# Retention and two FFN layers on one core: early steps in another order on GpSimd, ScalarE and VectorE

## The chip, the cores and the metric

The kernel runs on one core of one Trainium2 chip. The metric is the device time of one execution in microseconds; the median of three timed runs is used. A profile of one further execution gives the trace.

## The reference

The inputs q, k and v have 4 batches, 8 heads, 768 positions and 64 columns per head, in float32. A retention layer comes first, then two feed-forward layers without biases.

```
gamma = 1 - 2 ** (-5 - arange(H));  scale = 1 / sqrt(D)
for t in range(S):
    state = gamma * state + outer(k[t], v[t])
    y[t] = scale * q[t] @ state
x = y as (3072, 512)
h = x @ w_in;   x = max(0.01 * h, h) @ w_out           # 512 -> 2048 -> 512
h = x @ w2_in;  x = h * sigmoid(1.702 * h) @ w2_out
```

The weights arrive as 64-bit values and are turned into float32 on the chip.

## The kernel before

**Retention in chunks.** The positions are cut into chunks of 128. A step `s` is one chunk of one batch; there are 24, six to a batch (`c` is the chunk within its batch). `a_load(s)` fetches four rows of 256 KB: q transposed, k transposed, k by rows and v. `a_scale(s)` multiplies q by its decay on GpSimd (L298; on VectorE for step 0, L296). `a_scores(s)` makes the score matmuls (L278) and the mask product on VectorE (L281). For the steps below `TURNED` the rows of k are not loaded: TensorE transposes k (L286) and VectorE multiplies by the key decay (L289). For the other steps GpSimd does that product on the loaded rows (L300). The last chunk of a batch needs no rows of k. `a_out(s)` makes the state matmuls (L312), the values matmuls (L318), the matmuls with the carried state (L324) and the product that carries the state on (L327, VectorE, from PSUM). `a_store(s)` copies the output from PSUM (L340, ScalarE); for the first four steps, which are the first block of tokens of the FFN, it casts it (L343) and subtracts on GpSimd (L151), because the FFN works with a high and a low part of each float32.

**First FFN beside it.** From step `FIRST` = 6 on, three or four pieces of the first block's FFN run in every step (`ffn_pieces`, L229; three matmuls a contraction piece, four pieces for one of 16 column groups `m`). The weights of column group `m` pass through these instructions: the load of the raw words (`load_raw`, L161 and L163, sync queue), two on ScalarE (`words_scalar`, L173 and L174), four on VectorE (`words_vector`, L177, L179, L181, L183), a rounding addition on GpSimd (`round_up`, L192), the cast to the high part on ScalarE (L154) and the low part by subtraction on VectorE (L151), the last two in `finish`. `starts[m]` is the step whose pieces first use `m` (6, 7, 8, 9, 10, 11, 13, ...); the words are made two steps ahead of it and `finish` comes one step ahead. The raw words have a ring of three places, the made words a ring of two, the step inputs a ring of four.

**Order.** Every engine and every DMA queue runs its instructions in the order in which the program lists them. The order of the steps' parts is written out by hand in the loop at the end of `retention`. Everything after retention (the other blocks of the first FFN, its output layer and the second FFN) does not change.

**Start.** `qdec`, the decay of q, is made from two short rows (`qrows`) with one product on TensorE (L380) and copied by ScalarE (L381). `keep_warm` issues matmuls on zeros (L376), whose result nobody uses.

Of the kernel before, what the change touches and what calls it, by code (L numbers as in the profile page):

```python
# [11 lines left out]
F32 = mybir.dt.float32  # L12
BF16 = mybir.dt.bfloat16
F32R = mybir.dt.float32r
U32 = mybir.dt.uint32
# [6 lines left out]
P = 128  # L22
# [65 lines left out]
def retention_two_ffn(ctx: ExitStack, tc: tile.TileContext, qkv, consts, small, w1i, w1o, w2i, w2o, scratch, out):  # L88
    nc = tc.nc
# [21 lines left out]
    def ring(places, *dims):  # L111
        while True:
            for area, at in places:
                yield area.view(at, *dims)

    def run_of(area, n, step, at=0):
        return [(area, at + step * k) for k in range(n)]
# [22 lines left out]
    x0 = xs_a[0].view(0, NP, 2, TB)  # L140
# [6 lines left out]
    a_ring = ring(run_of(early, 2, 2), 512)  # L147
    raw, conv, wt = {}, {}, {}

    def subtract(o, x, y, e=nc.vector):  # L150
        e.tensor_tensor(out=o, in0=x, in1=y, op=ALU.subtract)  # L151

    def split(hi, lo, src, eng=nc.vector):
        nc.scalar.copy(out=hi, in_=src)  # L154
        subtract(lo, src, hi.bitcast(F32), eng)
# [3 lines left out]
    def exchanged(d, s):  # L159

        nc.sync.dma_start(out=d[:, :2], in_=s[:, :2])  # L161
        for r, t in halves:
            nc.sync.dma_start(out=d[r, 2:], in_=s[t, 2:])  # L163

    def load_raw(m):
        raw[m] = t = next(raw_ring).bitcast(U32)
        exchanged(t.rearrange("p (k f) two -> p k f two", k=NP),
                  w1i[m].bitcast(U32).rearrange("p (k f two) -> p k f two", k=NP, two=2))

    def words_scalar(f, low, high):  # L170


        nc.scalar.activation(out=f.bitcast(F32), in_=high.bitcast(F32), func=AF.Abs)  # L173
        nc.scalar.activation(out=low.bitcast(I32), in_=low, func=AF.Copy, scale=2.0**-29)  # L174
# [11 lines left out]
    def words(f, low, high):  # L186
        words_scalar(f, low, high)
        for step in words_vector:
            step(f, high)

    def round_up(f, low, e=nc.vector):
        e.tensor_tensor(out=f.bitcast(I32), in0=f.bitcast(I32), in1=low.bitcast(I32), op=ALU.add)  # L192

    def convert(m):
        t = raw.pop(m)
        a = next(a_ring).bitcast(U32)
        words(a, t[:, :, 0], t[:, :, 1])
        conv[m] = a, t[:, :, 0]

    def finish(m):  # L200
        a = conv.pop(m)[0].bitcast(F32)
        wt[m] = t = home["h1"].view(4 * m, 2, 512)
        split(t[:, 0], t[:, 1], a)
# [8 lines left out]
            x_load(q + 1)  # L212

    PIECES = NP * KF
    FIRST, TURNED = 6, 6
    upto = [PIECES * max(s - FIRST + 1, 0) // (N_STEPS - FIRST) for s in range(N_STEPS)]
    starts = [next(s for s in range(N_STEPS) if upto[s] > NP * m) for m in range(KF)]

# [24 lines left out]
    def retention():  # L243
# [5 lines left out]
        smalls = few.view(3, NC * H + NC * NP)  # L249
# [6 lines left out]
        gdec = smalls[:, NC * H :].rearrange("p (c n) -> p c n", c=NC)  # L256
        mask = mask_t.rearrange("p (n e) i -> p e n i", e=2)
        steps = [(b, c) for b in range(B) for c in range(NC)]
        ins, sc_t = {}, {}
        kv = banks[:, 2, : NP * D].rearrange("p (n d) -> p n d", n=NP)  # L260
        turned = banks[:, 7]
        o = banks[:, 3:5]
# [1 line left out]
        def a_load(s):  # L264
            ins[s] = next(in_ring)
            parts = ((0, 2), (3, 4)) if s < TURNED or steps[s][1] == NC - 1 else ((0, 4),)
            for a, b in parts:
                nc.sync.dma_start(out=ins[s][:, a:b], in_=qkv[s, :, a:b])
# [23 lines left out]
        def a_scale(s):  # L292
            b, c = steps[s]
            q, k = ins[s][:, 0], ins[s][:, 2].rearrange("p (h d) -> p h d", h=H)
            if s == 0:
                nc.vector.tensor_tensor(out=q, in0=q, in1=banks[:, 3], op=ALU.mult)  # L296
            else:
                nc.gpsimd.tensor_tensor(out=q, in0=q, in1=qdec, op=ALU.mult)  # L298
            if s >= TURNED and c < NC - 1:
                nc.gpsimd.tensor_tensor(out=k, in0=k, in1=kdec[:, c].unsqueeze(2).to_broadcast([P, H, D]), op=ALU.mult)  # L300

        def a_out(s):
            b, c = steps[s]
            t = ins.pop(s)
            sm, ks = sc_t.pop(s), t[:, 2].rearrange("p (h d) -> p h d", h=H)
            q = t[:, 0].rearrange("p (n i) -> p n i", n=NP)
            v = t[:, 3].rearrange("p (n f) -> p n f", n=NP)
            if c < NC - 1:
                for n in range(NP):
                    for e in range(2):  # L310
                        r = slice(D * e, D * e + D)
                        nc.tensor.matmul(out=kv[r, n], lhsT=ks[:, 2 * n + e], rhs=v[:, n, r],  # L312
                                         start=(c == 0 and n == 0), stop=True, skip_group_check=True)
            out = lambda n, e: o[D * (e ^ (n >> 1)) : D * (e ^ (n >> 1)) + D, n // 2, n % 2 * P : n % 2 * P + P]
            for n in (0, 2, 1, 3):
                for e in range(2):
                    r = slice(D * e, D * e + D)
                    nc.tensor.matmul(out=out(n, e), lhsT=v[:, n, r], rhs=sm[:, e, n], start=(n % 2 == 0),  # L318
                                     stop=(c == 0), skip_group_check=True)
            if c > 0:  # L320
                for n in (0, 2, 1, 3):
                    for e in range(2):
                        r = slice(D * e, D * e + D)
                        nc.tensor.matmul(out=out(n, e), lhsT=st[c % 2][r, n], rhs=q[r, n], start=False, stop=True,  # L324
                                         skip_group_check=True)
            if c < NC - 1:
                nc.vector.tensor_tensor(out=st[(c + 1) % 2], in0=kv, op=ALU.mult,  # L327
                                        in1=gdec[:, c + 1, :].unsqueeze(2).to_broadcast([P, NP, D]))

        def a_store(s):  # L330
            blk, cc = divmod(s, CPB)
            cols = slice(cc * P, cc * P + P)
            if blk == 1:
                x = x_raw[:, cc // 2, :, cc % 2 * P : cc % 2 * P + P]
            else:
                if cc % 2 == 0:
                    a_store.x = next(x_ring)
                x = a_store.x[:, :, cc % 2 * P : cc % 2 * P + P]

            nc.scalar.copy(out=x.rearrange("p (u m) i -> p u m i", u=2),  # L340
                           in_=o[:, :, : 2 * P].rearrange("p u (m i) -> p u m i", i=P))
            if blk == 0:
                nc.scalar.copy(out=x0[:, :, 0, cols], in_=x)  # L343
                subtract(x0[:, :, 1, cols], x, x0[:, :, 0, cols].bitcast(F32), nc.gpsimd)
            elif blk > 1 and cc % 2:
                nc.sync.dma_start(out=xd0[blk][:, cc // 2], in_=a_store.x)

        ins[0] = next(in_ring)
        nc.scalar.dma_start(out=qrows, in_=consts[0:P:D, H:].rearrange("p n i -> p (n i)"))
        nc.scalar.dma_start(out=smalls, in_=small)  # L350
        nc.sync.dma_start(out=ins[0][:, :2], in_=qkv[0, :, :2])
        nc.sync.dma_start(out=ins[0][:, 3:], in_=qkv[0, :, 3:])
        for n in (1, 2, 3):
# [19 lines left out]
        def keep_warm(n):  # L373

            for _ in range(n):
                nc.tensor.matmul(out=warm, lhsT=idle[:, :P], rhs=idle, start=True, stop=True, skip_group_check=True)  # L376

        pieces = itertools.chain.from_iterable(ffn_pieces(0, m) for m in range(KF))
        keep_warm(4)
        nc.tensor.matmul(out=banks[:, 3], lhsT=half, rhs=qrows, start=True, stop=True, skip_group_check=True)  # L380
        nc.scalar.copy(out=qdec, in_=banks[:, 3])  # L381
        keep_warm(4)
        a_scale(0)
        a_scores(0)
        a_scale(1)
        for s in range(len(steps)):
            if s == 0:
                keep_warm(4)
            if s < FIRST - 1:
                a_scores(s + 1)  # L390
            elif s >= FIRST:
                a_scores(s)
            for m in range(KF):
                if starts[m] == s + 1:
                    finish(m)
            fresh = [m for m in range(KF) if starts[m] == s + 2]
            for m in fresh:
                if m + 2 < KF:
                    load_raw(m + 2)
                convert(m)  # L400
            for _ in range(upto[s] - (upto[s - 1] if s else 0)):
                next(pieces)
            a_out(s)
            for m in fresh:
                round_up(*conv[m], nc.gpsimd)
            if s + 2 < len(steps):
                a_scale(s + 2)
            a_store(s)
            if s + 4 < len(steps):
                a_load(s + 4)  # L410
            if s == 1:
                load_raw(1)
            if s >= len(steps) - 4:
                x_split(1, s - len(steps) + 4)

# [712 lines left out]
```

## Time and profile before

| | |
|---|---|
| timed runs, median (lowest to highest) | 1053.87 us (1053.57 to 1054.02) |
| the profiled execution's own time | 1054.79 us |
| its span | 1053.0 us |
| TensorE busy | 1043.2 us, 99% |
| VectorE busy | 815.4 us, 77% |
| ScalarE busy | 552.7 us, 52% |
| GpSimd busy | 141.4 us, 13% |

The span is the time from the first to the last recorded instruction; the execution's own time has a little around it. Busy times are sums of the records of an engine. Matmuls are pipelined and their ends are modelled, so a busy TensorE is not TensorE at its peak. GpSimd works in the first 126 us, in retention, and again roughly between 580 and 790 us.

### The profile page before, as it was taken

The page shows a single profiled execution, that of the slowest core. Times are in us where ns is not written, and L with a number is a line of the kernel's source. Part 1 is how long each engine was busy: PE and PEld are TensorE (multiplying, and loading weights), DVE is VectorE, ACT ScalarE, POOL GpSimd, SP SyncE. Part 2 cuts the span into 40 slices and gives each one's busy share as a digit, 9 for nine tenths or more (in the row PEclk, how much of TensorE's full clock was granted, in tenths as well). Part 3 has the DMA queues.
Part 4 walks back from the last instruction along what each step waited for, and adds up shares of the span by engine and source line. Part 5 has one row for each costly group of instructions (what it writes and reads, how often), then busy time and mean ns, then how long its engine had stood idle before and what let it go on. Part 6 is the DMA issues. An engine that isn't in the chain of part 4 may idle for free.

```text
span 1053.0 us, 16918 instructions
## 1 busy us (share of the span) xinstructions
PE 1043.2 (99%) x5969; PEld 895.2 (85%) x5969; DVE 815.4 (77%) x1377; ACT 552.7 (52%) x976; POOL 141.4 (13%) x132
## 2 busy tenths in 40 slices
PE   9899999999999999999999999999999999999998
PEld 6677788888788888888888999999999888888886
DVE  4888739877796698788789667676777998887886
ACT  2444436554554554554555666565556564545443
POOL 4666500000000000000000203443510000000000
PEclk9999999999999999999999999999999999999999
DMA  7899667898896523623528855657578735726624
GB/s 256 281 342 363 242 202 236 285 340 304 301 344 237 186 63 108 229 80 130 191 71 310 288 194 184 237 194 257 181 249 269 262 101 128 193 86 150 165 81 80
DMA packets 168185, 221.11 MB, mean 210 GB/s; under 512 B 57634, under 2 KB 109090, under 8 KB 165668
## 3 DMA queue, kind: packets, MB, share of 16 engines
q1 hardware_dynamic: 133232, 173.05, 51.1%
q10 hardware_dynamic: 34868, 46.98, 12.2%
q8 instruction: 47, 0.77, 0.3%
q14 instruction: 38, 0.31, 0.1%
HBM read 135.05 MB, written 84.93 MB: 209 GB/s over the span
## 4 chain that ended last, share of the span: by engine, by line
PE 90%; DMA 4%; DVE 3%; ACT 1%; issue 1%; POOL 1%; ACTq 0%; SPq 0%; DVEq 0%; POOLq 0%
PE psum L786 41%; PE psum L593 22%; PE psum L229 21%; PE psum L278 2%; PE psum L318 2%; DMA wds<-b 2%; DMA h<-qkv 1%; PE psum L324 1%; PE psum L312 1%; DMA wds<-c 1%; PE psum L376 0%; DMA y<-c 0%; DVE b L151 0%; DVE c L1002 0%; DVE c L794 0%
## 5 line engine op out<-in xcount | busy, mean ns | idle before, releaser
L786 PE MATMUL psum<-c,h 128*128 128x512 f32 x1008 | 228.8, 389 | 0.0
L786 PEld LDWEIGHTS psum<-c,h 128*128 128x128 f32 x1008 | 189.3, 188 | 39.2
L786 PE MATMUL psum<-e,h 128*128 128x512 f32 x768 | 179.3, 389 | 0.0
L786 PEld LDWEIGHTS psum<-e,h 128*128 128x128 f32 x768 | 144.1, 188 | 29.9
L229 PE MATMUL psum<-d,h 128*128 128x512 f32 x576 | 136.8, 394 | 0.8 <-ACT e L234 0.8
L229 PE MATMUL psum<-a,h 128*128 128x512 f32 x576 | 131.2, 389 | 0.0
L229 PEld LDWEIGHTS psum<-d,h 128*128 128x128 f32 x576 | 106.7, 188 | 25.1 <-ACT e L234 1.2
L229 PEld LDWEIGHTS psum<-a,h 128*128 128x128 f32 x576 | 108.0, 188 | 22.6 <-issue 0.2
L593 PE MATMUL psum<-c,h 128*128 128x384 f32 x576 | 110.1, 334 | 0.3 <-DVE d L630 0.3
L593 PE MATMUL psum<-b,h 128*128 128x384 f32 x576 | 110.0, 334 | 0.0
L593 PEld LDWEIGHTS psum<-c,h 128*128 128x128 f32 x576 | 100.7, 188 | 0.6 <-DVE d L630 0.6
L593 PEld LDWEIGHTS psum<-b,h 128*128 128x128 f32 x576 | 100.8, 188 | 0.0
L739 ACT CAST c<-b 128x512 fp32r<-128x512 f32 x96 | 59.2, 622 | 57.1 <-DVE c L151 35.6
L613 ACT ACTIVATE d<-psum 128x384 f32<-128x384 f32 x96 | 47.1, 491 | 65.4 <-PE psum L593 57.7
L151 POOL TENSOR_TENSOR a<-a 128x768 f32<-128x768 f32 x7 | 13.2, 1893 | 498.5 <-DMA h<-wds 451.9
L151 DVE TENSOR_TENSOR c<-b,c 128x512 fp32r<-128x512 f32 x96 | 65.4, 689 | 18.8 <-ACT c L739 16.6
L739 ACT CAST e<-a 128x512 fp32r<-128x512 f32 x77 | 47.7, 622 | 43.8 <-PE psum L786 23.0
L234 ACT ACTIVATE e<-psum 128x512 f32<-128x512 f32 x80 | 47.5, 593 | 41.2 <-PE psum L229 38.4
L151 DVE TENSOR_TENSOR h<-h 128x384 fp32r<-128x384 f32 (+3 forms) x88 | 44.0, 535 | 27.7 <-ACT h L154 19.5
L151 DVE TENSOR_TENSOR e<-a,e 128x512 fp32r<-128x512 f32 x77 | 52.2, 684 | 8.3 <-ACT e L739 7.7
L617 DVE TENSOR_TENSOR d<-psum,d 128x384 f32<-128x384 f32 x96 | 52.0, 548 | 3.5 <-ACT d L613 2.7
L786 PE MATMUL psum<-f,h 128*128 128x512 f32 x192 | 48.7, 389 | 0.0
(157 smaller groups left out, 1470.4 us busy)
## 6 DMA issues: line engine op xcount, KB each, us to landing
gd<-d ACTq DMA_DIRECT2D x128, 192.0 KB, 3.7
gd<-e ACTq DMA_DIRECT2D x80, 256.0 KB, 5.2
d<-gd SPq DMA_DIRECT2D x64, 256.0 KB, 4.0
b<-gd SPq DMA_DIRECT2D x64, 256.0 KB, 4.0
h<-qkv SPq DMA_DIRECT2D x15, 1024.0 KB, 8.7
a<-gd SPq DMA_DIRECT2D x48, 256.0 KB, 5.2
xd<-e SPq DMA_DIRECT2D x12, 512.0 KB, 3.1
a<-xd SPq DMA_DIRECT2D x4, 1536.0 KB, 8.0
```

The lines of the kernel that those rows point to most:

```text
L151: e.tensor_tensor(out=o, in0=x, in1=y, op=ALU.subtract)
L229: nc.tensor.matmul(out=h, lhsT=w[:, a, k], rhs=xs[blk % 2][k][:, c], start=(i == 0), stop=(i == 3 * NP - 1), skip_group_check=True)
L234: nc.scalar.activation(out=t, in_=h, func=AF.Lrelu)
L278: nc.tensor.matmul(out=ps[:, e, n], lhsT=kT[r, n], rhs=qT[r, n], start=True, stop=True, skip_group_check=True)
L312: nc.tensor.matmul(out=kv[r, n], lhsT=ks[:, 2 * n + e], rhs=v[:, n, r], start=(c == 0 and n == 0), stop=True, skip_group_check=True)
L318: nc.tensor.matmul(out=out(n, e), lhsT=v[:, n, r], rhs=sm[:, e, n], start=(n % 2 == 0), stop=(c == 0), skip_group_check=True)
L324: nc.tensor.matmul(out=out(n, e), lhsT=st[c % 2][r, n], rhs=q[r, n], start=False, stop=True, skip_group_check=True)
L593: nc.tensor.matmul(out=t, lhsT=w[:, k, a], rhs=x[:, b, k], start=(start and m == 0), stop=(m == 5), skip_group_check=True)
L613: nc.scalar.activation(out=s, in_=src, func=AF.Sigmoid, scale=1.702)
L617: nc.vector.tensor_tensor(out=dst, in0=src, in1=s, op=ALU.mult)
L739: nc.scalar.copy(out=t[:, 0], in_=self.block_of(*item))
L786: nc.tensor.matmul(out=t[:, j], lhsT=w[:, j, a], rhs=x[:, b], start=(new and q == 0 and m == 0), stop=(q == NQ - 1 and m == 2), skip_group ...
```

## The change

- At the start, the small table of decays is fetched before the two decay rows. Eight spare matmuls stand before the decay product (four before), none between it and step 0 (four before) and three at the head of the loop (four before).
- `TURNED` is 3: steps 3 and 4 load the rows of k and have them multiplied on GpSimd.
- The parts of the first block are made two steps at a time (`a_parts`): a cast of 128x1024 on ScalarE and a subtraction, after step 3 on GpSimd (steps 0 and 1) and after step 4 on VectorE (steps 2 and 3).
- `a_scale(s + 2)` comes before the pieces and `a_out` in steps 0 to 5 and after `a_store` from step 6 on.
- `convert` issues only the two ScalarE instructions; the four of VectorE (`convert_rest`) come after `a_out`, so behind the state product. The rounding addition comes in the next step, just ahead of `finish`.

```diff
     def convert(m):
+        t = raw[m]
+        a = next(a_ring).bitcast(U32)
+        words_scalar(a, t[:, :, 0], t[:, :, 1])
+        conv[m] = a, t[:, :, 0]
+
+    def convert_rest(m):
         t = raw.pop(m)
-        a = next(a_ring).bitcast(U32)
-        words(a, t[:, :, 0], t[:, :, 1])
-        conv[m] = a, t[:, :, 0]
+        for step in words_vector:
+            step(conv[m][0], t[:, :, 1])
...
-    FIRST, TURNED = 6, 6
+    FIRST, TURNED = 6, 3
...
+        def a_rest(s):
+            if s + 2 < len(steps):
+                a_scale(s + 2)
...
                 if cc % 2 == 0:
                     a_store.x = next(x_ring)
+                    x_first.append(a_store.x)
...
-            if blk == 0:
-                nc.scalar.copy(out=x0[:, :, 0, cols], in_=x)
-                subtract(x0[:, :, 1, cols], x, x0[:, :, 0, cols].bitcast(F32), nc.gpsimd)
-            elif blk > 1 and cc % 2:
+            if blk > 1 and cc % 2:
                 nc.sync.dma_start(out=xd0[blk][:, cc // 2], in_=a_store.x)
 
+        def a_parts(u, e):
+            x = x_first[u]
+            t = x0[:, :, :, u * 2 * P : u * 2 * P + 2 * P]
+            nc.scalar.copy(out=t[:, :, 0], in_=x)
+            subtract(t[:, :, 1], x, t[:, :, 0].bitcast(F32), e)
+
         ins[0] = next(in_ring)
+        nc.scalar.dma_start(out=smalls, in_=small)
         nc.scalar.dma_start(out=qrows, in_=consts[0:P:D, H:].rearrange("p n i -> p (n i)"))
-        nc.scalar.dma_start(out=smalls, in_=small)
...
-        keep_warm(4)
+        keep_warm(8)
         nc.tensor.matmul(out=banks[:, 3], lhsT=half, rhs=qrows, start=True, stop=True, skip_group_check=True)
         nc.scalar.copy(out=qdec, in_=banks[:, 3])
-        keep_warm(4)
         a_scale(0)
         a_scores(0)
         a_scale(1)
         for s in range(len(steps)):
             if s == 0:
-                keep_warm(4)
+                keep_warm(3)
...
                 if starts[m] == s + 1:
+                    round_up(*conv[m], nc.gpsimd)
                     finish(m)
             fresh = [m for m in range(KF) if starts[m] == s + 2]
+            if s < FIRST:
+                a_rest(s)
...
             a_out(s)
             for m in fresh:
-                round_up(*conv[m], nc.gpsimd)
-            if s + 2 < len(steps):
-                a_scale(s + 2)
+                convert_rest(m)
             a_store(s)
+            if s >= FIRST:
+                a_rest(s)
             if s + 4 < len(steps):
                 a_load(s + 4)
             if s == 1:
                 load_raw(1)
+            if s in (3, 4):
+                a_parts(s - 3, (nc.gpsimd, nc.vector)[s - 3])
```

## Rows read from the trace of the kernel before

**Rows 1.** Engine line of the page: busy us, share of the span, instructions.
```profile
PE 1043.2 (99%) x5969; PEld 895.2 (85%) x5969; DVE 815.4 (77%) x1377; ACT 552.7 (52%) x976; POOL 141.4 (13%) x132
```
**Rows 2.** Timeline of TensorE, first 36 us: start, us, operation, tiles, [idle before].
```profile
1.26 1.89 PE L376 MATMUL psum<-f 128*128 128x512 bf16 x4 [1.26 <-DVE f L357]
3.08 2.07 PE L380 MATMUL psum<-b,f 2*128 2x512 f32 x2
...
6.90 2.08 PE L278 MATMUL psum<-h 64*128 64x128 f32 x16
8.91 1.04 PE L286 MATMUL psum<-f,h 128*128 128x128 f32 x4
...
10.74 1.16 PE L278 MATMUL psum<-h 64*128 64x128 f32 x16
...
17.90 1.16 PE L278 MATMUL psum<-h 64*128 64x128 f32 x16 [0.16 <-POOL h L298]
...
25.68 1.16 PE L278 MATMUL psum<-h 64*128 64x128 f32 x16 [0.15 <-POOL h L298]
...
28.26 0.67 PE L324 MATMUL psum<-h,b 64*64 64x128 f32 x16
...
32.71 1.16 PE L278 MATMUL psum<-h 64*128 64x128 f32 x16 [1.38 <-POOL h L298]
```
**Rows 3.** Timeline of TensorE, 32 to 140 us.
```profile
37.19 1.09 PE L318 MATMUL psum<-b,h 128*64 128x128 f32 x16 [0.43 <-DVE b L281]
...
62.86 1.16 PE L278 MATMUL psum<-h 64*128 64x128 f32 x16
...
79.57 1.16 PE L278 MATMUL psum<-h 64*128 64x128 f32 x16
...
85.72 1.16 PE L278 MATMUL psum<-h 64*128 64x128 f32 x16
...
91.18 1.16 PE L278 MATMUL psum<-h 64*128 64x128 f32 x16
```
**Rows 4.** Timeline of all engines: first q scaling, and a word activation.
```profile
5.80 0.69 DVE L296 TENSOR_TENSOR h<-h,psum 128x512 f32<-128x512 f32 x1 [4.60 <-ACT f L381]
...
27.34 0.69 ACT L174 ACTIVATE c<-c 128x512 int32<-128x512 uint32 x1
```
**Rows 5.** Timelines of VectorE and GpSimd, 28 to 42 us, put in order.
```profile
28.03 0.45 DVE L177 TENSOR_SCALAR c<-c 128x512 uint32<-128x512 uint32 x1
...
30.14 1.29 POOL L192 TENSOR_TENSOR b<-b,c 128x512 int32<-128x512 int32 x1 [1.94 <-DVE b L183]
...
37.29 1.29 POOL L298 TENSOR_TENSOR h<-h,f 128x512 f32<-128x512 f32 x1
...
38.02 1.11 DVE L151 TENSOR_TENSOR h<-b,h 128x512 fp32r<-128x512 f32 x1 [0.98 <-ACT h L154]
...
38.52 1.51 POOL L300 TENSOR_TENSOR h<-h,f 128x512 f32<-128x512 f32 x1
...
39.05 1.26 DVE L177 TENSOR_SCALAR c<-c 128x512 uint32<-128x512 uint32 x1
...
41.97 1.30 POOL L192 TENSOR_TENSOR b<-b,c 128x512 int32<-128x512 int32 x1 [1.94 <-DMA c<-w1i]
```
**Rows 6.** Timelines of GpSimd and VectorE near 688 us.
```profile
687.20 1.92 POOL L561 TENSOR_TENSOR a<-a 128x768 f32<-128x768 f32 x1
...
687.79 1.60 DVE L179 TENSOR_SCALAR e<-e 128x512 f32<-128x512 f32 x1
```
**Rows 7.** Groups of 0 to 60 us, GpSimd's groups, DMA issues of 17 to 22 us.
```profile
L281 DVE TENSOR_TENSOR b<-psum,b 128x1024 f32<-128x1024 f32 x11 | 13.4, 1220 | 10.0 <-PE psum L278 10.0
L327 DVE TENSOR_TENSOR b<-psum,f 128x256 f32<-128x256 f32 x9 | 3.7, 416 | 0.0
...
L151 POOL TENSOR_TENSOR a<-a 128x768 f32<-128x768 f32 x7 | 13.2, 1893 | 498.5 <-DMA h<-wds 451.9 <-DVE b L151 46.6
...
h<-qkv SPq DMA_DIRECT2D x1, 1024.0 KB, 6.4
```

More of the change, by code (lines that the diff above doesn't have):

```diff
@@ L258, in retention @@
         steps = [(b, c) for b in range(B) for c in range(NC)]
-        ins, sc_t = {}, {}
+        ins, sc_t, x_first = {}, {}, []
         kv = banks[:, 2, : NP * D].rearrange("p (n d) -> p n d", n=NP)
```

## Prediction

> **What bounds the kernel now.** The engine line first: TensorE is busy 99% of the span [rows 1], so only idle TensorE, or TensorE at its lower clock, can be won. The early steps are therefore read next, from the starts of the score matmuls, one set a step [rows 2]; sc(s) stands for the scores of step s.
>
> Three things are to be seen there. The 16 matmuls of sc(0) take 2.08 us, those of sc(1) 1.16. [...] From sc(1) to sc(3) are 7.16 us, 0.16 of it a wait for GpSimd's scaling of q, so 7.0 of work. A step without transposes is 25.68 to the end of 28.26, 3.2 us. And sc(6) starts after 1.38 us of waiting for GpSimd.
>
> Then the later steps [rows 3]. Where nothing waits, a step with four FFN pieces is 6.15 us (79.57 to 85.72) and one with three is 5.46 (85.72 to 91.18). From sc(6) at 32.71 to sc(11) at 62.86 are 30.15 us; a first step without the carried state costs 4.9 (5.46 less about 0.6) and the other four 2x6.15+2x5.46, together 28.1. So 2.1 us are lost in steps 6 to 10. The wait before the values matmul at 37.19 names who: VectorE.
>
> Last, VectorE beside GpSimd [rows 5]. The weight's first word step (L177) takes 0.45 us at 28.03 but 1.26 at 39.05, where GpSimd's L300 ends at 40.03: it runs 0.28 after that end. L151 is held the same way until L298 ends at 38.58, and then needs 0.55; L300, queued at 38.52, gets its turn when L151 ends (39.13) and needs 0.90 more, although VectorE had L177 waiting. So these instructions exclude each other and take turns. The same shows between L179 and L561 late in the kernel [rows 6]: 1.60 us, ending 0.27 after L561. VectorE's products out of PSUM are not held: L327 and L281 have means of 0.42 and 1.22 with GpSimd beside them [rows 7].
>
> **Part by part.** *Start.* Four spare matmuls span 1.89 us, 0.43 apart; eight put the decay product from 3.08 to about 4.7. From its start to the end of the first q scaling were 2.07, the copy until 5.80 and 0.69, for VectorE waits for ScalarE's copy [rows 4]: 3.4, so sc(0) at 8.15, not 6.90. The four spares that filled this gap are gone. At the lower clock until 9.5, sc(0) ends at 9.85; transposes 0.58, three spares 0.65: sc(1) at 11.07 against 10.74, +0.3. Bounds: with the higher clock from about 5 on it is 9.4 (-1.7 beside this); with none until the transposes are through, or with the decay rows landing late behind the small table, 12.4 (+1.3). [...]
>
> [...]
>
> *Steps 1 to 5.* GpSimd loses four subtractions (about 1.3 each, as L298) and with them the waits of the scores; steps 3 and 4 lose their transposes. sc(3) = 11.07+7.0, then two steps of 3.2: step 3 ends at E = 24.4, before at 25.6. Steps 3 and 4 load 256 KB more each, and load 4, now one transfer, starts only when step 0 has used its values (14.2). From an idle queue I take 5 us, 19.2; scaling 1.3: ready at 20.5 for sc(4) at 21.3. With the 6.4 us of the 1 MB load in rows 7 it is 21.9: +0.6. Loads 5 and 6 (issued at 18.1 and 21.3) come before their scalings. The two key products on GpSimd, 0.90 each, lie in its idle time.
>
> *The first weights.* Here the gain is lost. ScalarE: after step 3's output copy (0.55) comes the two-step cast; a word activation over 512 elements takes 0.69 [rows 4], so it is between that and 1.4, I take 1.03. Then the two word activations, done at E+2.7 = 27.1 (before 28.03). GpSimd begins the two-step subtraction at E+1.6 = 26.0; 1.89 for 768 elements [rows 7] and 1.29 for 512 make 2.5: until 28.5 (from below, 1.9). VectorE's L177, ready at 27.1, waits until 28.5 and ends at 28.8. GpSimd now has step 6's q and k scaling queued ahead of the weight's addition, so turns are taken: q 1.14 to 29.9, L179 0.28 to 30.2, k 0.90 to 31.1, L181 to 31.4, L183 to 32.0. Next in VectorE's order is its own two-step subtraction, twice 0.55, until 33.1; GpSimd's addition (L192) until 34.2, where before it ran from 30.14 to 31.43. Cast 0.65: 34.9; q of step 7 until 35.4; L151 0.55: 36.0. sc(6) is over at 31.1, so TensorE waits 3.8 us for the first weights. VectorE goes on: k of step 7 until 36.9, L177 0.28, three more 1.55, mask product 1.2: the values matmul of step 6 at 39.95 against 37.19 [rows 3]: **+2.75**.
>
> *Steps 6 to 10.* The round from L192 over cast, L151 and the word steps to the next L192 is 5.92 us (30.14 to 41.97, two rounds). The state product L327 now stands between L151 and L177; it costs nothing as long as GpSimd's k scaling holds L177 for 0.90 anyway. Without that cover, 0.42 x 5 = 2.1 more. That the addition now comes in the next step changes no order within the round. TensorE's own step, 5.8 in the mean, takes back 0.25: +2.5 at step 10. Raw weights 3 and 4 wait on the sync queue for the later addition (34.2 for 31.43), and load 9 behind them; its scaling comes only at 46.
>
> *After step 10* TensorE alone sets the pace with VectorE's mask products over 1.5 us ahead, which hides the new order; were that cover gone, 0.42 a step. The rest of the kernel is untouched.
>
> Sum: +0.3 at the start, -1.5 in the early steps, +3.95 at the first weights, -0.25 later: +2.5. The profiled execution took 1054.79 (span 1053.0 and 1.8 around it) and would become 1057.3; it lies 0.9 above the median of 1053.87, from which I predict **1056.4**.
>
> **Rivals.** *(a) Early clock.* The eight spares raise it, and everything moves 1.7 us ahead: +0.8, 1054.7. [...] Against: four spares and the decay product did not. 0.18.
>
> *(b) Clock lost or late.* [...] Against: after 1.38 us idle, sc(6) still took 1.16 [rows 2]. 0.14. [...]
>
> *(c) Other sign: VectorE isn't held.* If the word steps run beside GpSimd's, L183 ends at 29.1, GpSimd's addition at 32.1, L151 at 33.5; the values matmul starts at 36.65 (-0.55), and the round shrinks to 5.1, below TensorE's step, so the losses after it in steps 6 to 10 (1.55 of the 2.1) come back too: -2.1, 1051.8, and below it with any help from the clock. It decides from a first L183 ending before 29.5. Against: rows 5 and 6. For: they don't show three ready VectorE steps against two GpSimd ones. 0.20.
>
> *(d) It cancels.* The two-step parts come earlier than I place them (the lower bound of the subtraction, another turn): 0 to +1.5, 1054.6. 0.12.
>
> **Numbers.** The forecast has 0.36. A change under 0.2% (2.1 us) can't be told from none here. Slower takes the forecast and (b): 0.50. Faster takes two thirds of (c): 0.14. Same takes (a), (d) and the rest of (c): 0.36. The range leaves out the far part of (b) and the far third of (c): 1051.4 to 1058.4; the forecast's own, by the bounds of start and loads, is 1055.5 to 1057.7.
>
> **What would show it.** Step 3 ends near 24.4 and no scores wait for GpSimd before sc(6); L177 at about 27 lasts 1.7 us, L179 and L181 over 1 us each; the first FFN matmul comes near 35 after a gap of over 3 us; sc(11) near 65.3. It is wrong with sc(1) far from 11, a first L183 before 30, or waits past step 11.

## The result and the profile after

The changed kernel takes 1062.24 us (median of 4, 1060.54 to 1063.14) against 1053.94 for the kernel before, measured beside it: ratio 1.0074, interval 1.0056 to 1.0092. It is slower, as forecast, but by 8.3 us instead of the forecast 2.5, and outside the range. Three single executions of the experiments below and of the kernel before (1485.68, 1742.85 and 3416.77 us) ran far slower than all others of the same kernel and are left out of every number. The changed kernel's profiled execution took 1061.51 us with a span of 1059.8, 6.8 more than the span before; those 6.8 are what has to be placed.

TensorE's timeline of the changed kernel names the places (start, us, operation, tiles, idle before it and what ended the idle time). Against the kernel before, L389 is its L376 (spares), L393 its L380 (decay product), L283 its L278 (scores), L321 its L312 (state), L291 its L286 (transposes), L327 its L318 (values), L234 its L229 (FFN pieces). L303 and L305 are GpSimd's scalings of q and k (L298, L300 before), L286 is VectorE's mask product, L192 still the rounding addition:

```profile
1.25 3.59 PE L389 MATMUL psum<-f 128*128 128x512 bf16 x8 [1.25 <-DVE f L370]
5.03 2.04 PE L393 MATMUL psum<-b,f 2*128 2x512 f32 x2 [0.18 <-DMA b<-consts]
8.46 2.08 PE L283 MATMUL psum<-h 64*128 64x128 f32 x16 [1.40 <-DVE h L301]
10.47 1.11 PE L291 MATMUL psum<-f,h 128*128 128x128 f32 x4
11.38 1.49 PE L389 MATMUL psum<-f 128*128 128x512 bf16 x3
12.80 1.58 PE L283 MATMUL psum<-h 64*128 64x128 f32 x16
...
26.51 1.16 PE L283 MATMUL psum<-h 64*128 64x128 f32 x16
...
32.49 1.16 PE L283 MATMUL psum<-h 64*128 64x128 f32 x16 [0.33 <-POOL h L303]
37.14 0.86 PE L234 MATMUL psum<-d,h 128*128 128x512 f32 x2 [3.49 <-ACT h L154]
38.27 3.13 PE L234 MATMUL psum<-d,h 128*128 128x512 f32 x7 [0.28 <-DVE h L151]
...
42.20 1.09 PE L327 MATMUL psum<-b,h 128*64 128x128 f32 x16 [0.18 <-DVE b L286]
43.23 1.16 PE L283 MATMUL psum<-h 64*128 64x128 f32 x16
...
67.30 1.16 PE L283 MATMUL psum<-h 64*128 64x128 f32 x16
...
144.77 1.43 PE L234 MATMUL psum<-a,h 128*128 128x512 f32 x5
```

Two more rows of the kernel before are needed for the sum, its scores of step 7 and the first FFN pieces of the second block:

```profile
38.64 1.16 PE L278 MATMUL psum<-h 64*128 64x128 f32 x16 [0.35 <-POOL h L298]
...
136.84 2.34 PE L229 MATMUL psum<-a,h 128*128 128x512 f32 x9
```

With sc(1) at 12.80, sc(5) at 26.51 and sc(11) at 67.30 in the changed kernel, and the starts of [rows 2, 3], the 6.8 us come out by stretch:

| stretch | before | after | difference | forecast |
|---|---|---|---|---|
| start of span to sc(1) | 10.74 | 12.80 | +2.06 | +0.3 |
| sc(1) to sc(5) | 14.94 | 13.71 | -1.23 | -1.5 |
| sc(5) to sc(7), the first weights | 12.96 | 16.72 | +3.76 | +3.95 |
| sc(7) to sc(11) | 24.22 | 24.07 | -0.15 | -0.25 |
| sc(11) to the second block's pieces | 73.98 | 77.47 | +3.49 | 0 |
| from there to the end | 916.16 | 915.03 | -1.13 | 0 |
| sum | 1053.0 | 1059.8 | +6.80 | +2.5 |

Two terms are wrong, the first and the fifth. (Of the -1.13, 0.8 is one wait of L229 for ScalarE's L234, which the kernel before has in the rest of its span and the changed one has not.) The first weights went as worked out, in all but one instruction. The timeline of all engines of the changed kernel from 28 us on, of which VectorE and GpSimd are shown:

```profile
28.25 2.37 POOL L151 TENSOR_TENSOR d<-h,d 128x1024 fp32r<-128x1024 f32 x1 [3.14 <-ACT d L358]
...
29.19 1.73 DVE L177 TENSOR_SCALAR c<-c 128x512 uint32<-128x512 uint32 x1
...
31.17 1.27 POOL L303 TENSOR_TENSOR h<-h,f 128x512 f32<-128x512 f32 x1 [0.54 <-DMA h<-qkv]
31.28 1.44 DVE L181 TENSOR_SCALAR b<-b 128x512 uint32<-128x512 uint32 x1
...
32.39 1.22 POOL L305 TENSOR_TENSOR h<-h,f 128x512 f32<-128x512 f32 x1
...
32.75 1.41 DVE L183 SCALAR_TENSOR_TENSOR b<-b,c 128x512 uint32<-128x512 uint32 x1
...
34.30 2.14 POOL L192 TENSOR_TENSOR b<-b,c 128x512 int32<-128x512 int32 x1 [0.68 <-issue]
```

L177 ends 0.30 behind the two-step subtraction, L181 and L183 0.28 and 0.55 behind L303 and L305: the word steps of 0.42 to 0.69 us take 1.4 to 1.7, because each waits for the GpSimd instruction that has its turn. (L179 alone, forecast over 1 us, took 0.41: GpSimd was waiting for the load of step 6 then.) The words end at 34.16, 7.65 behind sc(5); the forecast had 7.6 (32.0 behind 24.4). The values matmul stands 15.7 behind sc(5); the forecast had 15.55.

The waits of TensorE in the first 146 us of the changed kernel (total, times, longest):

```profile
PE psum L234 <- ACT h L154: 3.5, 1, 3.5
PE psum L327 <- DVE b L286: 2.6, 6, 0.8
PE psum L283 <- DVE h L301: 1.4, 1, 1.4
```

The second row is the one that the prediction excluded: six waits for VectorE's mask product, three of them past step 11 (at 94.87, 118.17 and 137.48, together 1.96). By the starts of the scores, the 3.49 us of the fifth stretch lie in steps 14, 15, 17, 19 and 22 (0.36, 0.53, 0.18, 1.02 and 1.59 us longer than before); the other steps there are together 0.19 shorter.

### The profile page after: what moved, and what is told of

It reads as the page before. It is cut to its first block, busy times and chain, and to the rows that moved or that the text cites. A ratio compares the mean times of both kernels' runs of the same rounds, so it can differ in the third digit from the quotient of the medians.

```text
span 1059.8 us, 16891 instructions
## 1 busy us (share of the span) xinstructions
PE 1044.9 (99%) x5960; PEld 896.0 (85%) x5960; DVE 815.1 (77%) x1376; ACT 552.0 (52%) x974; POOL 141.4 (13%) x131
## 4 chain that ended last, share of the span: by engine, by line
PE 91%; DMA 4%; DVE 1%; issue 1%; POOL 1%; ACT 1%; SPq 0%; ACTq 0%; POOLq 0%; DVEq 0%
PE psum L803 43%; PE psum L234 22%; PE psum L610 22%; DMA h<-qkv 3%; PE psum L283 1%; PE psum L327 1%; DMA gd<-e 1%; PE psum L333 1%; POOL b L192 0%; POOL h L305 0%; PE psum L321 0%; DMA b<-consts 0%; DVE b L286 0%; PE psum L291 0%; DVE b L183 0%
## 5 line engine op out<-in xcount | busy, mean ns | idle before, releaser
L234 PE MATMUL psum<-d,h 128*128 128x512 f32 x576 | 138.3, 397 | 4.0 <-ACT h L154 3.5
L234 PEld LDWEIGHTS psum<-d,h 128*128 128x128 f32 x576 | 107.5, 189 | 29.1 <-ACT h L154 3.7
L234 PE MATMUL psum<-a,h 128*128 128x512 f32 x576 | 131.2, 389 | 0.0
L234 PEld LDWEIGHTS psum<-a,h 128*128 128x128 f32 x576 | 108.0, 188 | 22.6 <-issue 0.2
```

The source lines that it names most:

```text
L234: nc.tensor.matmul(out=h, lhsT=w[:, a, k], rhs=xs[blk % 2][k][:, c], start=(i == 0), stop=(i == 3 * NP - 1), skip_group_check=True)
```

## The experiments

Times are medians; the kernel before, run beside each of them, was at 1053.9 to 1054.7. sc(s) are starts of score matmuls in the profiled execution.

**The start undone.** The changed kernel with the four, four and four spares and the order of the two small loads as before.

```
...
-        keep_warm(8)
+        keep_warm(4)
...
+        keep_warm(4)
         a_scale(0)
...
```

> The changed kernel with the start as before: decay rows fetched first, spare matmuls 4, 4 and 4. Theory (the gap without spare matmuls between the decay product and step 0 keeps TensorE at its lower clock until about 13): the scores of step 1 start at 10.7 in place of 12.8, step 3 ends near 24.2, the first values matmul of step 6 near 39.8 in place of 42.2, and the time falls by 2 us, to about 1060. Rival (later waits set the pace anyway): the scores of step 1 move, but the time stays at 1062.

1060.5 us, ratio 1.0053 (1.0035 to 1.0072). sc(1) at 11.21 and sc(5) at 24.51: the forecast 24.4 for sc(5) holds with the old start. But only 1.29 of the 2.0 us reach sc(7) (41.94). The windows of 5 us (us, busy time of PE, PEld, DVE, ACT and POOL, granted clock, DMA share, GB/s) show TensorE at its lower level:

```profile
30.00:35.00 5.00, 1.25 (x24) 0.97 (x16) 3.30 (x4) 0.47 (x1) 3.86 (x4) 0.96 0.93 267
35.00:40.00 5.00, 4.79 (x16) 3.03 (x17) 4.75 (x6) 1.77 (x4) 3.06 (x3) 0.50 0.82 274
```

The nine pieces of step 6 follow an idle stretch of 3.95 us and take 4.49, where they took 2.33 to 2.37 at the upper level; sc(5) to sc(7) is 17.43, not 16.72. So rival (b), the clock lost in the gap, happens, and here it costs about 0.7: VectorE's mask product of step 6 ends at 40.13, but the state matmuls, at 1.12 us instead of 0.69, hold the values matmul until 40.53, and that one takes 1.48 instead of 1.09.

**The addition ahead of the scaling again.** From step 6 on the rounding addition (L192) goes back to its own step, in front of GpSimd's scaling.

```
...
                 convert_rest(m)
+                if s >= FIRST:
+                    round_up(*conv[m], nc.gpsimd)
```

> The changed kernel with the rounding addition of a weight back in the step that makes its words, ahead of GpSimd's scaling, from step 6 on; all else as changed. Theory (from step 11 on the addition stands behind a scaling that waits for its load): scores of step 11 stay at 67.3, but the later waits go and the second block starts 3.5 us earlier, at 141.3; time about 1058.7. Rival (VectorE's words behind the state product are what is late): waits and time stay within 0.5 us of the changed kernel.

1057.66 us, ratio 1.0029 (1.0017 to 1.004): 4.6 us come back, the largest single part. GpSimd's timeline shows why. In the changed kernel, late in the first block's pieces:

```profile
121.78 1.29 POOL L303 TENSOR_TENSOR h<-h,f 128x512 f32<-128x512 f32 x1 [3.48 <-DMA h<-qkv]
...
128.08 1.30 POOL L303 TENSOR_TENSOR h<-h,f 128x512 f32<-128x512 f32 x1 [4.00 <-DMA h<-qkv]
129.33 1.05 POOL L305 TENSOR_TENSOR h<-h,f 128x512 f32<-128x512 f32 x1
130.33 1.30 POOL L192 TENSOR_TENSOR b<-b,c 128x512 int32<-128x512 int32 x1
...
131.66 0.62 ACT L154 CAST h<-b 128x512 fp32r<-128x512 f32 x1 [4.50 <-POOL b L192]
...
136.12 1.22 DVE L286 TENSOR_TENSOR b<-psum,b 128x1024 f32<-128x1024 f32 x1
137.48 1.09 PE L327 MATMUL psum<-b,h 128*64 128x128 f32 x16 [0.84 <-DVE b L286]
```

The scaling stands first and waits 4.00 us for its load; the addition behind it needs nothing of that load, and ScalarE's cast waits 4.50 for the addition. In the kernel with the addition first:

```profile
124.23 1.29 POOL L192 TENSOR_TENSOR b<-b,c 128x512 int32<-128x512 int32 x1 [3.98 <-ACT h L350]
125.49 1.75 POOL L303 TENSOR_TENSOR h<-h,f 128x512 f32<-128x512 f32 x1
...
130.65 1.64 POOL L192 TENSOR_TENSOR b<-b,c 128x512 int32<-128x512 int32 x1 [1.94 <-ACT a L154]
```

The scaling no longer finds its load late, and TensorE waits for the mask product once (0.5 us). From sc(11) to sc(23) are 68.55 us, as before the change (68.30).

That the loads come on time again points to a loop. A raw weight is loaded (L161) into a place that an addition has to free, and the loads of q, k and v stand behind it in the sync queue. So a late addition makes a later load late, and that load holds a later scaling, with the next addition behind it. The waits from 62 to 135 us (total, times, longest) in the changed kernel:

```profile
POOL h L303 <- DMA h<-qkv: 12.3, 4, 4.0
SPq L161 <- POOL b L192: 8.9, 3, 3.2
```

In the kernel before:

```profile
POOL h L298 <- DMA h<-qkv: 2.4, 3, 1.5
SPq L161 <- POOL b L192: 2.2, 3, 1.0
```

With the addition first, the scaling has no such wait. The rows at 128.08 to 137.48 show the whole way from a late load to the wait in step 22. From 85 us to the wait at 118.17, in step 19, no scaling waits for a load; that this loss has the same cause is shown by this run, not by those rows, and the loop itself is read from the traces and not tried alone.

**VectorE's words ahead of the pieces again.** The rival to the last: the new order on VectorE is at fault.

```
                 convert(m)
+                if s >= FIRST:
+                    convert_rest(m)
...
```

> The changed kernel with VectorE's four word instructions back ahead of the pieces and of the state product from step 6 on; the addition stays in the next step, behind the scaling. Theory (the addition behind the scaling is the cause): under 1 us of the 3.5 us lost after step 11 comes back, 1061.5 or more. Rival (VectorE's order is the cause): all 3.5 us come back, 1058.7.

1061.29 us (three executions, 1059.92 to 1064.65), ratio 1.0069 (1.0047 to 1.0092), as the changed kernel; there is no trace to read. The rival's 1058.7 us would be a ratio of 1.0043, outside the interval. So the order on VectorE is not the cause of the 3.5 us. The interval leaves room for a smaller share, but the run before this one has VectorE's order as changed, and its sc(11) to sc(23) is within 0.25 us of the kernel before.

**The scaling of steps 6 and 7 behind the first two additions,** which go back to their own steps for it.

```
...
-            if s < FIRST:
+            if s < FIRST - 2:
                 a_rest(s)
...
+                if s < FIRST:
+                    round_up(*conv[m], nc.gpsimd)
...
```

> The changed kernel with GpSimd's scaling of steps 6 and 7 behind the first two weights' additions again (early scaling only in steps 0 to 3); the two-step parts stay. Theory (VectorE's word instructions take turns with the two scalings of step 6): the last word instruction of the first weight ends 1.7 us earlier against the end of step 3, the values matmul of step 6 starts near 40.5 in place of 42.2, time about 1060.5. Rival (the two-step subtractions alone make the first weights late): less than 0.5 us.

1061.22 us, ratio 1.0064 (1.0049 to 1.0079): a small gain, less than expected. The words end 5.92 behind sc(5) instead of 7.65, but L192 still takes 2.14 us beside VectorE's two-step subtraction, and now sc(6) pays:

```profile
36.70 1.56 PE L283 MATMUL psum<-h 64*128 64x128 f32 x16 [3.83 <-POOL h L303]
38.19 3.50 PE L234 MATMUL psum<-d,h 128*128 128x512 f32 x9
```

The idle stretch has moved from the pieces to the scores; sc(5) to sc(7) is 15.88 (16.72).

**The gap at the start filled.** Four more spares between decay product and step 0, where TensorE was idle for 1.40 us.

```
+        keep_warm(4)
         a_scale(0)
```

> The changed kernel with four more spare matmuls between the decay product and step 0, where TensorE was idle for 1.4 us. Theory (that gap keeps TensorE at its lower clock until about 13): the higher clock comes near 9.5 as in the kernel before, the scores of step 0 stay at 8.5, those of step 1 start near 11.1 in place of 12.8, time 1.5 us less. Rival (the clock rises when it does, whatever TensorE is given): scores of step 1 at 12.8, time unchanged.

1062.04 us, ratio 1.0073 (1.005 to 1.0095): nothing. sc(1) is at 13.01, although TensorE works from 1.25 on with no pause but the 0.19 us that the decay product waits for its rows. The gap is not what delays the start:

```profile
5.04 2.04 PE L393 MATMUL psum<-b,f 2*128 2x512 f32 x2 [0.19 <-DMA b<-consts]
...
8.82 2.08 PE L283 MATMUL psum<-h 64*128 64x128 f32 x16
...
11.74 1.34 PE L389 MATMUL psum<-f 128*128 128x512 bf16 x3
13.01 1.16 PE L283 MATMUL psum<-h 64*128 64x128 f32 x16
```

**Spares in the wait for the first weights.** Sixteen spare matmuls behind the scores of step 6.

```
+            if s == FIRST:
+                keep_warm(16)
```

> The changed kernel with 16 spare matmuls behind the scores of step 6, where TensorE waits 3.5 to 4 us for the first weights. Theory (the wait drops the clock, but VectorE's mask product of step 6 ends at 42.1 anyway): the granted clock stays at 1.00 in 35 to 40, the pieces of step 6 end near 40 in place of 41.3, the scores of step 7 start at 43.1 as before, time within 0.5 us of the changed kernel. Rival (the lower clock is what step 6 costs): scores of step 7 near 41.8 and time 1.4 us less.

1061.32 us, ratio 1.0069 (1.0053 to 1.0084), no gain that can be told. The granted clock stays 1.00 from 30 to 45 us, and yet:

```profile
35.91 0.81 PE L234 MATMUL psum<-d,h 128*128 128x512 f32 x2
37.01 1.88 PE L234 MATMUL psum<-d,h 128*128 128x512 f32 x7 [0.29 <-DVE h L151]
38.82 0.69 PE L321 MATMUL psum<-h 128*64 128x64 f32 x16
40.94 1.09 PE L327 MATMUL psum<-b,h 128*64 128x128 f32 x16 [1.44 <-DVE b L286]
```

What the faster pieces win, the values matmul waits for VectorE: sc(5) to sc(7) is 16.86 (16.72). In the changed kernel the loss of the clock lies in VectorE's shadow.

**One-step parts on GpSimd again.** The two-step cast and subtractions are undone.

```
...
+            if blk == 0:
+                nc.scalar.copy(out=x0[:, :, 0, cols], in_=x)
+                subtract(x0[:, :, 1, cols], x, x0[:, :, 0, cols].bitcast(F32), nc.gpsimd)
...
-            if s in (3, 4):
-                a_parts(s - 3, (nc.gpsimd, nc.vector)[s - 3])
...
```

> The changed kernel with the parts of the first block made one step at a time again, all subtractions on GpSimd. Theory (the two-step subtractions hold VectorE's words and GpSimd's addition): the last word instruction of the first weight ends 3 us earlier against the end of step 3, but the addition still stands behind the scaling of step 6, so the first low part is ready 1.6 us earlier; scores of step 7 near 41.6, time 1.6 us less. Rival (the load of step 6 sets the scaling and so the addition, whatever the parts do): less than 0.5 us.

1060.54 us, ratio 1.0059 (1.0045 to 1.0073). sc(5) to sc(7) is 15.08: the two-step parts carry 1.6 of the 3.76. Against that sc(1) to sc(5) is 14.51 again (13.71), with 0.9 us of scores waiting for GpSimd.

**Each weight one step earlier.** An attempt to do better: start and parts as before, three steps' keys turned, raw weight 1 loaded at the start, each conversion a step earlier, scores of step 6 issued in step 5.

```
...
-                if starts[m] == s + 1:
+                if starts[m] == s + 2:
...
-            fresh = [m for m in range(KF) if starts[m] == s + 2]
+            fresh = [m for m in range(KF) if starts[m] == s + 3]
...
```

> A version built from the findings: start and one-step parts as before the change; loaded keys from step 3 (in two transfers, the second raw weight fetched at the start) and early scaling in steps 0 to 5 as in the change; each weight made one step earlier than in either kernel, the addition in the same step ahead of the scaling, VectorE's words ahead of the state product from step 6 on; the scores of step 6 issued in step 5. Theory (first weights ready before the pieces of step 6, so TensorE never waits 2 us there): first FFN matmul near 31, scores of step 11 near 59 against 62.9 in the kernel before, time about 1050.5. Rival (VectorE and GpSimd, taking turns, are the bound of steps 4 to 10 in any order): scores of step 11 at 61.5 to 63, time 1052.5 to 1054.

1056.81 us, ratio 1.0022 (1.0013 to 1.0031): slower than before, a miss. The values matmul of step 5 waits 2.23 us for ScalarE's output copy (L350), which stands behind the cast and the word activations of an early weight, and the state matmuls of step 7 wait 1.74 for the state product of the step before. It traded one wait for two.

**The start alone,** on the kernel before: eight, none and three spares, the small table loaded ahead of the decay rows.

```
...
-        keep_warm(4)
+        keep_warm(8)
...
-        keep_warm(4)
         a_scale(0)
...
```

> The kernel before with the change's start alone: eight spare matmuls, the decay product, none, step 0, three; the small constants loaded ahead of the query rows. Theory (the start term of my sum was mis-sized, and it is a term of its own): the scores of step 1 start at 12.8 us, as in the changed kernel, not at 10.74, those of step 5 at about 27.5, and the time is 1054.1 + 2 = 1056.1. Rival (the late start is absorbed by the 2.0 us that the early scores of the kernel before spend waiting for GpSimd's scaling): step 1 at 12.8, step 5 at 25.7 to 26, time 1054.1 to 1054.5.

1056.29 us, ratio 1.0019 (1.001 to 1.0028): +2.1. sc(1) is at 12.82, sc(5) 27.91, sc(11) 65.08, each 2.1 to 2.2 behind [rows 2, 3]; nothing absorbs it. The start is a term of its own, +2.1. It has two parts that no run separates. The eight spares end at 4.84; and the decay rows, fetched second, are there only at about 5.0: in six of the seven traces with this start the decay product waits for them (DMA b<-consts, 0.18 to 0.64 us). Fetched first, they hold it in no trace, not even where it starts at 2.33. So with the loads in this order, four spares would have left the decay product at about 5.0 as well, if the rows land at the same time; that was not tried.

**No spares ahead of the decay product,** on the kernel before.

```
-        keep_warm(4)
         nc.tensor.matmul(out=banks[:, 3], lhsT=half, rhs=qrows, ...)
```

> The kernel before without the four spare matmuls ahead of the decay product; those behind it stay. [...] Rival (the clock counts all that TensorE did from 1.25 us on): without the four spares it rises later, step 1 starts at 12 us or later, time 1055 or more.

Expected was sc(1) no later than before, between 9.0 and 10.8, and 1052.5 to 1054.2 us. 1053.78 us, ratio 0.9994 (0.9985 to 1.0003): no difference. The decay product starts at 2.34, sc(0) at 6.13, sc(1) at 10.60. Without the four spares the clock is up about as early as with them. It does not come earlier with the decay product either: sc(0) is 0.77 ahead of the kernel before, sc(1) only 0.14, and the four spares at 9.05 still span 1.62 (1.03 in the kernel before).

**Three parts undone together:** start, parts and the place of the addition.

```
...
-        keep_warm(8)
+        keep_warm(4)
...
-            if s in (3, 4):
-                a_parts(s - 3, (nc.gpsimd, nc.vector)[s - 3])
...
                 convert_rest(m)
+                if s >= FIRST:
+                    round_up(*conv[m], nc.gpsimd)
```

> The changed kernel with three parts undone together: the start as before, the first block's parts one step at a time on GpSimd, and from step 6 on the rounding addition in its own step ahead of the scaling. What is left of the change is: keys of three steps turned, scaling ahead of the first weights' work, VectorE's words behind the pieces. Theory (the parts act as separate pieces of one schedule; the rest keeps a first weight about 15.1 us behind the scores of step 5, which now start at 24.5): the scores of step 7 start at 40.0 us against 38.64, step 11 at 64.2, and the time is 1054.1 + 1.4 = 1055.5. Rival 1 (what the single experiments gave back adds up: 1.74 + 4.58 + 1.70): 1054.2, equal to before. Rival 2 (part of what each gave back was the same microseconds): 1056.5 or more.

1055.09 us, ratio 1.001 (0.9999 to 1.0021): near the theory's 1055.5, and its interval takes in 1054.2 too. Of the 0.74% all but 0.1% is back. sc(7) is at 39.75, 1.11 behind the kernel before, and sc(5) to sc(7) 14.58: what is left is the scaling in front of the first addition. GpSimd there:

```profile
29.00 1.27 POOL L303 TENSOR_TENSOR h<-h,f 128x512 f32<-128x512 f32 x1 [1.36 <-DMA h<-qkv]
30.23 1.49 POOL L305 TENSOR_TENSOR h<-h,f 128x512 f32<-128x512 f32 x1
31.68 1.27 POOL L192 TENSOR_TENSOR b<-b,c 128x512 int32<-128x512 int32 x1
```

The addition begins at 31.68, 6.5 behind sc(5), when the scaling is through, although VectorE's words end at 30.81; before it was 30.14, 4.5 behind [rows 5].

**Three steps' keys alone,** on the kernel before, with the scaling of steps 2 to 5 ahead of the output's work.

```
-    FIRST, TURNED = 6, 6
+    FIRST, TURNED = 6, 3
...
+            if s < FIRST - 2:
+                a_scale(s + 2)
```

> The kernel before with the part of the change that my sum counted as a gain alone: keys of three steps turned, not six (those of steps 3 and 4 loaded in two halves), and the scaling of steps 2 to 5 ahead of the output's work; the scaling of steps 6 and 7, the words and the additions as before. Theory (the early scores no longer wait for GpSimd, and the first weight follows step 5 at the distance it had): step 5's scores start at 24.4, not 25.68, steps 6 to 11 1.0 to 1.3 us earlier, time 1052.6 to 1053.1. Rival (the first weight's conversion is paced by its own load and by VectorE, not by step 5): step 5 at 24.4, but the values matmul of step 6 at 37.2 as before, time 1054.1.

1053.65 us, ratio 0.9996 (0.9987 to 1.0005): the same. sc(1) to sc(5) is 14.42 against 14.94: half of the transposes' time is lost, since three scores now wait 0.9 us for a scaling that stands behind the one-step subtraction of the step before. In this trace sc(1) also came late, at 11.36, so that sc(5) is at 25.78 and not at 24.4.

**The same with the one-step subtractions on VectorE.**

```
-                subtract(x0[:, :, 1, cols], x, ..., nc.gpsimd)
+                subtract(x0[:, :, 1, cols], x, ..., nc.vector)
```

> The kernel before with the keys of three steps turned (steps 3 and 4 loaded in two halves), the scaling of steps 2 to 5 ahead of the output's work, and the first block's one-step subtractions on VectorE in place of GpSimd; start, words, additions and the scaling from step 6 on as before. Theory (what held the early scores in the kernel with the keys alone was the subtraction in front of the scaling in GpSimd's queue): no score of steps 2 to 5 waits for GpSimd, step 5's scores start at 24.4 to 24.7, step 7's at 37.4 to 37.8 (13.0 behind, as in the kernel before), and the time is 1054.1 - 1.1 = 1053.0, ratio 0.999. Rival 1 (the subtraction on VectorE now waits for ScalarE ahead of the mask product and passes the wait on): step 5 at 25.5 or later, time 1054.1. Rival 2 (step 5 is earlier but the first weight is paced by its own load and conversion): step 7 at 38.6, time 1054.1.

1053.87 us, ratio 0.9993 (0.9985 to 1.0002): the same again. No score up to sc(5) waits for GpSimd, and sc(1) to sc(5) is 13.75: the -1.2 exist. But more than half of the 0.8 by which sc(5) is ahead is gone at sc(7) (38.28 against 38.64): VectorE's words begin at 27.72 against 28.03, behind the subtraction and the mask product. Rival 2 of this run is nearer than its theory.

**And without the spares ahead of the decay product.**

```
-        keep_warm(4)
         nc.tensor.matmul(out=banks[:, 3], lhsT=half, rhs=qrows, ...)
```

> The same kernel without the four spare matmuls ahead of the decay product. Theory (those spares do nothing for the clock): the scores of step 1 start between 10.4 and 11.3 as in all kernels with four or none ahead, time within 0.4 us of the kernel with the four. Rival (they do, and the other run without them was an accident): step 1 at 12 or later, time 1 us more.

1052.58 us against 1054.44, ratio 0.9982 (0.9973 to 0.9991): 0.1 to 0.3% faster than before, and the best version found. sc(1) is at 10.49. Its lead over the kernel with the four spares (1.29) is more than the theory's 0.4, but it is not to be seen in the two traces, where sc(11) is at 62.57 and 62.53; the intervals overlap.

## Why the prediction was right in direction and wrong in size

**The start: mis-sized.** The step that failed is the start term of +0.3, which had the lower clock end at 9.5; it measured +2.06 in the changed kernel and +2.1 alone, beyond even the bound of 12.4 for sc(1). Of the 1.73 by which sc(1) missed 11.07, 0.31 is the decay product: it begins at 5.03, not 4.7, so that sc(0) is at 8.46 instead of 8.15. About 0.1 of that was a slip in the sum (four more spares at 0.43 make 4.8); the rest is mostly the wait for the decay rows, which the prediction had only in its bound. The other 1.4 is the clock. The granted clock reads 1.00 from 0 to 15 us in both kernels, so its level is read from the durations; in the run with the sixteen spares the same 2.08 of sc(0) and 1.11 of the transposes stand where it falls to 0.50 (8 to 11 us). I kept its rise at a time of day, as if the spares moved in front counted for it. In this start they don't: the three spares at 11.38 span 1.49, no faster than the four that span 1.89 in [rows 2], and a start with none in front is as good as one with four. (No run shows the rise at 9.5 that the sum uses. In the kernel before, the four transposes at 8.91 span 1.04, against 1.11 wholly at the lower level and 0.66 at the upper, the changed kernel's at 10.47 and 14.30, so the rise came near their end.) Keeping TensorE without a gap changed nothing either: the run with the gap filled has no pause but 0.19 us, and its three spares at 11.74 still span 1.34. What is shown is that the rise comes later with a later start (sc(1) at 12.65 to 13.01 in six of the seven traces with eight spares) instead of at a time of day, and that the four spares in front of the decay product bought nothing (sc(1) at 10.74 with them, at 10.60 without); rival (b)'s late clock came true. How much of the later start is the spares and how much the order of the loads is not shown. What the clock does count stays open: with one and the same start (the kernel before and five others) sc(1) came between 10.74 and 11.36, and in every trace read, wherever its spares stood, sc(0) took 2.08 us, so the rise that lasted came behind it.

**Early steps: right.** -1.23 against -1.5, and sc(5) came at 24.51 where the start was undone. The last two variants show that it needs both the turned keys and GpSimd's queue without subtractions.

**First weights: right, in mechanism and size.** The turns between VectorE and GpSimd came as listed but for L179, because load 6, which the prediction had ahead of its scaling, came 0.54 late; the sum of the stretch holds to 0.15 us over 15.7. Rival (c) falls: the first L183 ends 7.65 behind sc(5). Rival (d) falls too: the two-step subtraction took 2.37 (forecast 2.5, lower bound 1.9), and the stretch costs 3.76 of the forecast 3.95. Of the 3.76, 1.6 go with the two-step parts (16.72 less 15.08), and 1.6 stay with the scaling in front of the first addition (14.58 less 12.96; the kernel with three steps' keys alone, which scales behind it, takes 12.91). That kernel also has VectorE's words ahead of the pieces, so the 1.6 is put down to the scaling by the rows at 29.00 to 31.68 and not by a run that moves it alone. The last 0.5 was not told apart.

**Rival (b) in the gap:** the granted clock read 0.76 from 35 to 40 us in the changed kernel, behind 3.49 us of idle, and 0.50 with the old start, behind 3.95, so the clock is lost; with the sixteen spares in the wait it read 1.00. Shorter waits settle nothing: behind the 1.38 of [rows 2] the upper level stayed, and behind 1.64 with the subtractions on VectorE (nine pieces in 2.37); behind 1.65 in the last variant it did not (nine pieces in 3.91, a granted clock of 0.79 from 35 to 40 us), and in one trace the lower level came back around an idle of 1.40 us (last section). With the old start its price was about 0.7; in the changed kernel the spares in the wait bought nothing, as VectorE's chain ended later. What the range, up to 1058.4, takes in for it was my estimate, and no run shows it.

**After step 10: wrong.** "TensorE alone sets the pace with VectorE's mask products over 1.5 us ahead, which hides the new order" failed: +3.49, and 4.6 in the time. I looked for the cost of the order on VectorE, and it is not there. What the runs show in its place is GpSimd's queue: the change put the rounding addition behind the next step's scaling, and undoing that alone brings 4.6 us back. The rows show how: a scaling that waits for its load (4 times, 12.3 us) holds the addition behind it. For steps 6 to 10 I wrote that the addition in the next step "changes no order within the round"; that holds only while no load is late. The kernel before had such waits too (3 times, 2.4 us); with the addition in front of them, TensorE has no wait past step 8. The prediction did see that raw weights 3 and 4 wait in the sync queue for the later addition, and load 9 behind them, but it did not follow this past step 9.

**The rest.** With the start, the two-step parts and the addition's place undone, all but 1 us is back. I looked at each part's price for its own step, and missed the two places where a part changed what other work stood behind.

## What to carry to other kernels

An instruction that may wait for a transfer goes last among the instructions that are ready on its engine's queue: moved one place forward, it cost nothing from step 7 to step 10, where the loads were on time, and 3.5 us after step 10, where they were not. When a sum charges an edit only at the step it touches, look along the whole kernel for the waits that stood harmlessly behind other work on the same queue. An earlier start of a stage is worth only what the next chain lets through: where step 5 came 0.8 us earlier, step 7 came 0.36 earlier.

## Not expected of the hardware

In the run with the sixteen spares, whose start is that of the changed kernel, the clock rose and fell: the eight spares span 3.37 us in place of 3.59 and the decay product took 1.09 in place of 2.04, then came the 1.40 us of idle, and the scores of step 0 took 2.08 again. The granted clock of 5 to 10 us read 0.77, of 10 to 15 us 0.89:

```profile
1.25 3.37 PE L389 MATMUL psum<-f 128*128 128x512 bf16 x8 [1.25 <-DVE f L370]
5.26 1.09 PE L393 MATMUL psum<-b,f 2*128 2x512 f32 x2 [0.64 <-DMA b<-consts]
7.75 2.08 PE L283 MATMUL psum<-h 64*128 64x128 f32 x16 [1.40 <-DVE h L301]
```

So rival (a), the early clock, can happen as well: it did in one of the seven traces with eight spares, so spares in front can count, and even then it did not last to the first scores. Executions also differ more: the kernel with the gap filled ranged from 1058.84 to 1065.96 us in four, the kernel before beside it from 1052.81 to 1055.43 in fifteen. Why was not tried.
